# Squared-ReLU attention with top-128 routing on one Trainium2 core: transposing DMAs for two units of each of the last four batches instead of all units of two, and a new hand-written order

## The chip, the cores and the metric

The kernel runs on one core of a Trainium2 chip. The metric is device time in microseconds (us) of one execution; several executions give a median. Engines are named as the profile names them: PE (TensorE matmul), PEld (its weight loads), DVE (VectorE), ACT (ScalarE), POOL (GpSimd), SP (SyncE, which here issues DMAs alone).

## What is computed

Attention for 8 batches, 12 heads, 448 positions and 64 values a head, without a softmax: the scores are scaled, cut off below 0 and squared. Its result, laid out as 448 rows of 768, goes through a layer that treats 128 rows of each batch: those with the highest score against a gate vector.

```python
scores = scale * np.matmul(q, k.transpose(0, 1, 3, 2))
attn = np.maximum(scores, 0.0) ** 2 / S
x = np.matmul(attn, v)                      # then to (B, S, 768)
...
scores = np.einsum('bsd,d->bs', x, w_gate)
out = x.copy()
for b in range(B):
    top_idx = np.argpartition(-scores[b], capacity)[:capacity]   # capacity 128
    xe = x[b, top_idx]
    ye = np.maximum(xe @ w1, 0.0) @ w2
    g = 1.0 / (1.0 + np.exp(-scores[b, top_idx]))
    out[b, top_idx] = x[b, top_idx] + g[:, None] * ye
```

## The kernel before, in words

The work is cut into 24 units of four heads; units 3b, 3b+1 and 3b+2 make batch b. All engines' work is written out by hand in one string, `ORDER` (L535 to L622): each item is a name, a unit or batch, and PSUM banks or an engine. Every engine takes its own items in the order of that string, and waits by itself for the data and buffers that an item needs. PSUM has eight banks; all outputs of PE go through them, so that an item that writes to a bank waits until ACT or DVE has read what stood there.

For unit u:

- `L,q,u`, `L,k,u`, `L,v,u` (L106) load its queries, keys and values from POOL's queue. Six buffers of each kind stand ready. Units that are named in `BYDMA` (L45) are loaded with two DMAs of half the partitions each (L113), in another order of the heads; the others with one (L111).
- `T,u,0` and `T,u,1` (L226) turn queries and keys over on PE, 14 transposes each; `TE,u` (L240) brings both to SBUF, on DVE.
- `S,u,c` for c = 0 to 6 (L256): the scores, four matmuls with 64x64 tiles and 448 columns. `R,u,c` (L264): ReLU of the two banks, always on ACT, 128x896. `Q,u,0` and `Q,u,3` (L270): squares on DVE.
- `V,u,c` (L276): times the values, four matmuls again; `X,u` (L286) brings the result, transposed (768 x 448 for a batch), to `xT_sb`, on ACT or DVE.
- The rows of the output, `x_rows`, are that result turned back. Either `RT,u` does it on PE (L298: 8 transposes of 128x128, or 16 of half the width where a flag says so) and `RE,u` (L307) evicts it on ACT or DVE, or, for units in `BYDMA`, `XB,u` (L314) does it with two transposing DMAs on SP's queue, from SBUF to SBUF, without PE, ACT and DVE.
- `ST,b` (L324) stores a batch's rows from POOL's queue with two DMAs, once all three units of the batch are there.

For a batch b of 0 to 6: `colx`, `colE`, `bt`, `rk`, `cs`, `rank`, `hots`, `sel`, `sE` (L360 to L431) find the 128 rows; `XG` (L443, POOL) gathers them from the stored output, so that it waits for `ST,b`; `XT` and `xeE` turn them over; `h` and `hE` (L481, L492) are the first layer in eight parts, `y` and `yE` (L500, L509) the second; `gs` and `sig` make the gate; `ADD` (L517, POOL) adds to the output in DRAM. Batch 7 takes its rows from `x_rows` in SBUF by matmul (`xe`, L433). Some items have a flag for the width of their tile on PE: `h` and `y` with it do their work as two half tiles of 64 columns.

At the start (`LFq`, `LFk`, L118 and L121) the first queries and keys come by SP's queue in FP32: queries, then 2 of 7 parts of the keys, then the other 5. `Cq` and `Ck` (L201, L204) cast them, `T,0,0` and `TK` (L237) turn them over, `TQE` and `TKE` (L250, L253) bring them to SBUF; all queries go through one PSUM bank. `PW` (L207) are matmuls of zeros that fill PE's time.

Of the kernel before, what the change touches and what calls it, by code (L numbers as in the profile page):

```python
# [21 lines left out]
def kernel(  # L22
# [518 lines left out]
    TE,2,2,D S,2,0,0 R,2,0,A S,2,1,2 R,2,1,A X,0,D S,2,2,4 S,2,3,6 L,q,3 T,3,0,0 Q,1,3,7 T,3,1 TE,3,2,D R,2,2,A
    L,v,1 L,k,4 V,1,0,2 V,1,1 V,1,2 V,1,3 R,2,3,A S,2,4,4 S,2,5,6 S,2,6,0 Q,2,0,3 L,q,4 R,2,4,A V,1,4 V,1,5
    V,1,6 R,2,5,A R,2,6,A T,4,0,4 S,3,0,6 R,3,0,A X,1,D T,4,1 TE,4,2,D L,k,5 Q,2,3,7 S,3,1,0 S,3,2,2 S,3,3,6
    R,3,1,A S,3,4,4 L,v,2 L,q,5 T,5,0,0 T,5,1 R,3,2,A R,3,3,A S,3,5,2 R,3,4,A TE,5,2,D S,3,6,6 V,2,0,4 V,2,1
    L,q,6 R,3,5,A Q,3,0,3 Zk V,2,2 V,2,3 V,2,4 S,4,0,0 R,3,6,A R,4,0,A Q,3,3,7 S,4,1,2 L,k,6 L,k,7 L,v,3 W,0,3,6
    W,0,5,6 V,2,5 V,2,6 R,4,1,A S,4,2,6 X,2,A T,6,0,0 T,6,1 W,0,1,6 R,4,2,A TE,6,2,D RT,0,1,2 colx,0,0,3 S,4,3,4
    RE,0,D colx,0,1 colx,0,2 Q,4,0,3 R,4,3,A Zb colE,0 S,4,4,0 S,4,5,6 L,q,7 RT,1,0,2 RE,1,D R,4,4,A R,4,5,A
    RT,2,0,4 S,4,6,0 bt,0,5 RE,2,D rk,0,2 R,4,6,A L,q,8 L,v,4 Q,4,3,7 S,5,0,6 S,5,1,2 R,5,0,A R,5,1,A V,3,0,0
    rk,0,0 V,3,1 V,3,2 V,3,3 S,5,2,6 R,5,2,A rk,0,3 V,3,4 V,3,5 V,3,6 rk,0,1 L,k,8 X,3,A T,7,0,2 T,7,1 TE,7,2,D
    S,5,3,6 R,5,3,A S,5,4,0 S,5,5,4 cs0,0,6 cs,0,0 cs,0,1 R,5,4,A cs,0,2 Zx,1 rank,0 hots,0 R,5,5,A RT,3,0,7  # L550
    RE,3,D S,6,0,2 S,5,6,0 L,v,5 R,6,0,A sel,0,6 T,8,0,4 T,8,1 R,5,6,A Q,5,0,3 sE,0 S,6,1,2 R,6,1,A TE,8,2,D
    S,6,2,0 V,4,0,6 R,6,2,A V,4,1 V,4,2 V,4,3 S,6,3,2 R,6,3,A V,4,4 V,4,5 S,6,4,4 Q,5,3,7 V,4,6 R,6,4,A X,4,D
    L,k,9 V,5,0,0 V,5,1 Q,6,0,3 S,6,5,2 L,v,6 R,6,5,A V,5,2 V,5,3 S,6,6,4 R,6,6,A ST,0 Q,6,3,7 V,5,4 V,5,5 V,5,6
    X,5,A S,7,0,2 R,7,0,A colx,1,0,6 colx,1,1 S,7,1,4 RT,4,0,7 colx,1,2 R,7,1,A S,7,2,0 L,q,9 T,9,0,2 R,7,2,A
    W,0,4,6 T,9,1 W,1,0,8 colE,1 S,8,0,4 R,8,0,A L,k,10 L,q,10 bt,1,6 TE,9,2,D S,7,3,0 S,7,4,2 R,7,3,A R,7,4,A
    V,6,0,4 Zx,2 V,6,1 V,6,2 V,6,3 S,7,5,0 rk,1,3 R,7,5,A rk,1,0 V,6,4 V,6,5 V,6,6 S,8,1,2 RE,4,D L,q,12 Q,7,0,3
    RT,5,1,7 rk,1,2 rk,1,1 R,8,1,A X,6,A T,10,0,0 S,7,6,2 R,7,6,A XG,0 T,10,1 S,8,2,4 cs0,1,6 cs,1,0 W,0,2,6
    RE,5,D TE,10,2,D cs,1,1 cs,1,2 W,0,0,6 rank,1 XT,0,0,7 R,8,2,A S,8,3,2 R,8,3,A S,8,4,0 S,8,5,4 W,1,6,8 L,v,7
    xeE,0,2,D h,0,0,0,6 h,0,1,0 hots,1 R,8,4,A h,0,2,0 S,8,6,2 h,0,3,0 L,k,12 R,8,5,A R,8,6,A S,9,0,0 S,9,1,4
    Q,7,3,7 h,0,4,0 h,0,5,0 L,v,8 h,0,6,0 h,0,7,0 R,9,0,A R,9,1,A S,9,2,0 R,9,2,A V,7,0,2 Q,8,0,3 V,7,1 V,7,2  # L560
# [118 lines left out]
```

## Time and profile before

| what | us |
|---|---|
| median of 3 runs (197.3 to 199.45) | 197.46 |
| the profiled execution | 197.49 |
| span of its instructions in the trace | 195.8 |
| what lies outside the span | 1.69 |

Times in the trace count from the start of the span. The profile's page has the busy time of each engine, the chain of work that ended last, and the costliest groups of instructions; other views give busy time by stretch (windows), the instructions in order of time (timeline, which merges neighbours of one kind: its start is that of the first, and the step of one is the difference of two starts), and who waited for whom.

### The profile page before, as it was taken

To read this page: it belongs to the slowest core of one execution; us is meant where nothing else is said; L and a number is where in the kernel's file an instruction comes from. 1 tells how busy PE (TensorE), PEld (TensorE's weight loads), DVE (VectorE), ACT (ScalarE), POOL (GpSimd) and SP (SyncE) were. 2 spreads that over 40 slices of the span, in tenths; PEclk is the share of its full clock that TensorE was granted. 3 is DMA by queue.
4 is the path that set the end of the run, shared out by engine and by line. 5 is a ranking of instruction groups with operands and counts; after the bars stand their busy time and mean duration, and the time that the engine had idled before them with its cause. 6 is when DMAs were issued, how large, how long until landed. Compare 5 with 4: busy or idle time off the path is not lost.

```text
span 195.8 us, 7321 instructions
## 1 busy us (share of the span) xinstructions
PE 178.4 (91%) x3221; PEld 125.0 (64%) x3221; DVE 162.0 (83%) x228; ACT 164.4 (84%) x209; POOL 111.1 (57%) x160
## 2 busy tenths in 40 slices
...
GB/s 171 148 186 203 204 209 202 263 282 194 181 197 347 207 99 172 197 299 246 174 167 191 326 149 235 252 130 115 120 133 309 155 272 216 187 79 291 47 125 26
DMA packets 32333, 37.70 MB, mean 193 GB/s; under 512 B 8744, under 2 KB 29614, under 8 KB 31278
## 3 DMA queue, kind: packets, MB, share of 16 engines
...
## 4 chain that ended last, share of the span: by engine, by line
PE 61%; ACT 25%; issue 5%; DVE 4%; POOL 2%; POOLq 0%; DVEq 0%; ACTq 0%
ACT r_sb L216 24%; PE ps L260 12%; PE ps L487 10%; PE ps L505 10%; PE ps L281 9%; PE ps L233 7%; PE ps L295 4%; PE ps L209 2%; PE ps L365 2%; POOL out_dram L523 2%; PE ps L377 1%; DVE a_sb L274 1%; ACT xT_sb L216 1%; DVE qkt L220 1%; DVE mask_sb L388 1%
## 5 line engine op out<-in xcount | busy, mean ns | idle before, releaser
L216 ACT ACTIVATE r_sb<-ps 128x896 bf16<-128x896 f32 x168 | 140.2, 967 | 6.3 <-PE ps L260 5.8
L274 DVE TENSOR_TENSOR a_sb<-r_sb 128x2688 bf16<-128x2688 bf16 (+1 forms) x48 | 84.8, 1784 | 2.7 <-ACT r_sb L216 1.8
L260 PE MATMUL ps<-qkt 64*64 64x448 bf16 x672 | 55.5, 361 | 3.2 <-ACT r_sb L216 2.3
L281 PE MATMUL ps<-a_sb,v_sb 64*64 64x448 bf16 x672 | 41.7, 350 | 0.6 <-ACT r_sb L216 0.4
L260 PEld LDWEIGHTS <-qkt 64*64 64x64 bf16 x672 | 22.1, 104 | 21.1 <-issue 11.0
L220 DVE COPY qkt<-ps 128x1792 bf16<-128x1792 bf16 (+2 forms) x25 | 26.0, 1045 | 2.1 <-PE ps L233 1.6
L281 PEld LDWEIGHTS <-v_sb 64*64 64x64 bf16 x672 | 21.4, 107 | 9.3 <-issue 1.6
L446 POOL DMA_INDIRECT xg<-out_dram,idx x7 | 13.3, 1897 | 22.3 <-DVE idx L430 12.0
L487 PE MATMUL ps<-xeT,w_sb 128*128 128x128 bf16 (+1 forms) x396 | 24.6, 220 | 0.0
L487 PEld LDWEIGHTS <-w_sb 128*128 128x128 bf16 (+1 forms) x396 | 21.9, 98 | 4.0 <-issue 3.1
L505 PE MATMUL ps<-w_sb,hT 128*128 128x384 bf16 (+1 forms) x132 | 24.3, 327 | 0.0
L523 POOL DMA_INDIRECT out_dram<-gye,idx x9 | 17.4, 1929 | 8.6 <-ACT gye L216 6.6
L327 POOL DMA_DIRECT2D out_dram<-x_rows x8 | 4.5, 561 | 28.9 <-DMA x_rows<-xT_sb 9.2
L111 POOL DMA_DIRECT2D v_sb<-in_v_dram x18 | 14.0, 781 | 4.2 <-PE ps L260 1.8
L505 PEld LDWEIGHTS <-hT 128*128 128x128 bf16 (+1 forms) x132 | 11.1, 98 | 8.0 <-issue 2.1
L233 PE MATMUL ps<-ident,q_sb 128*64 128x128 bf16 x336 | 14.3, 225 | 1.6 <-ACT r_sb L216 1.2
L233 PEld LDWEIGHTS <-q_sb 128*64 128x64 bf16 x336 | 11.8, 112 | 6.3 <-issue 5.6
L222 DVE TENSOR_SCALAR xT_sb<-ps 128x896 bf16<-128x896 f32 x12 | 13.1, 1088 | 2.1 <-PE ps L281 1.2
L111 POOL DMA_DIRECT2D q_sb<-in_q_dram x17 | 12.9, 757 | 3.0 <-DVE a_sb L274 1.2
L233 PE MATMUL ps<-ident,k_sb 128*64 128x128 bf16 x336 | 14.1, 221 | 0.0
L111 POOL DMA_DIRECT2D k_sb<-in_k_dram x17 | 12.6, 741 | 2.2 <-PE ps L260 1.4
L216 ACT ACTIVATE xT_sb<-ps 128x896 bf16<-128x896 f32 x12 | 11.7, 975 | 0.8 <-PE ps L281 0.8
(122 smaller groups left out, 200.4 us busy)
## 6 DMA issues: line engine op xcount, KB each, us to landing
...
```

The lines of the kernel that those rows point to most:

```text
L111: nc.gpsimd.dma_start(out=dst, in_=src(t, u))
L216: nc.scalar.activation(out=out_, in_=in_, func=func or AF.Copy, scale=scale)
L220: nc.vector.tensor_copy(out=out_, in_=in_)
L222: nc.vector.tensor_scalar(out=out_, in0=in_, scalar1=scale, scalar2=None, op0=ALU.mult)
L233: nc.tensor.matmul(out=PSB[HALF[j], at["T", u, w], n * 128:(n + 1) * 128], lhsT=s[:, j, c, :], rhs=ident, is_transpose=True, start=(n == 0 ...
L260: nc.tensor.matmul(out=PS[HALF[hf], bank + j, :S], lhsT=qkt[u][HALF[j], 1, c, hf, :], rhs=qkt[u][HALF[j], 0, :, hf, :], start=True, stop=True)
L274: nc.vector.tensor_tensor(out=a_sb[u][:, c0:c1], in0=r, in1=r, op=ALU.mult)
L281: nc.tensor.matmul(out=PS[HALF[j], at["V", u] + hf, :S], lhsT=v_sb[u % NBUF][HALF[hf], j, c, :], rhs=a_sb[u][HALF[hf], c, j, :], start=(c ...
L446: read = reads[self.b] = nc.gpsimd.indirect_dma_start(out=self.xg, out_offset=None, in_=out[0:self.b + 1].rearrange("b s d -> (b s) d"), i ...
L487: nc.tensor.matmul(out=PS[p, self.at["h"] + bk, o:o + 128], lhsT=w1_sb[:, m, f * 128 + p.start:f * 128 + p.stop], rhs=self.xeT[:, m, :], s ...
L505: nc.tensor.matmul(out=PS[p, self.at["y"] + w, :384], lhsT=self.hT[:, f, p], rhs=w2_sb[:, f, w * 384:(w + 1) * 384], start=(f == 0), stop= ...
L523: add = nc.gpsimd.indirect_dma_start(out=out[0:self.b + 1].rearrange("b s (w d) -> (b s w) d", w=w), out_offset=bass.IndirectOffsetOnAxis( ...
```

## The change

Eight units instead of six have their rows turned by DMA: the first two of each of batches 4 to 7 (12, 13, 15, 16, 18, 19, 21, 22), where before all of batches 5 and 6 did (15 to 20). The units in `BYDMA` are also those that are loaded by halves. The first queries are turned over into two PSUM banks: five of seven parts into one, two into another, and the two are evicted apart, the first on ACT. Of the loads by SP the first keys now come ahead of the queries. The whole order is written anew, with other banks, other engines for some evictions, and other places for half tiles.

```diff
-    BYDMA = (15,16,17,18,19,20)
+    BYDMA = (12,13,15,16,18,19,21,22)
...
+    NA = 5
...
+        if (u, w, n0) == (0, 0, 0):
+            n1 = NA
+        o = NA if (u, w, n0) == (0, 0, NA) else 0
         for n in range(n0, n1):
             c = n // 2 + NR * (n % 2) if w == 0 else n
             for j in range(2):
-                nc.tensor.matmul(out=PSB[HALF[j], at["T", u, w], n * 128:(n + 1) * 128],
+                nc.tensor.matmul(out=PSB[HALF[j], bank if o else at["T", u, w], (n - o) * 128:(n - o + 1) * 128],
                                  lhsT=s[:, j, c, :], rhs=ident, is_transpose=True,
-                                 start=(n == 0), stop=(n == NC - 1), skip_group_check=True)
+                                 start=(n == o), stop=(n == n1 - 1 if (u, w) == (0, 0) else n == NC - 1),
+                                 skip_group_check=True)
+
+    def TB(bank):
+        at["TB"] = bank
+        T(0, 0, bank, NA, NC)
...
-            put(eng, flat[:, w, n0 * 128:n1 * 128], PSB[:, at["T", u, w], n0 * 128:n1 * 128])
+            own = (u, w, n0) == (0, 0, NA)
+            put(eng, flat[:, w, n0 * 128:n1 * 128],
+                PSB[:, at["TB"], :(n1 - n0) * 128] if own else PSB[:, at["T", u, w], n0 * 128:n1 * 128])
...
-    Zz PW,32,0 Zi Zs LFq Cq,0 Zt LFk,0,2 Zm Ck,0,2,D Cq,1 T,0,0,0 TK,0,2 LFk,2,7 TQE,0,7,D Ck,2,7,D TKE,0,2,A
+    Zz PW,32,0 Zi Zs LFk,0,2 Zh Zt Zm LFq Cq,1 Cq,0 LFk,2,7 PW,6,1 T,0,0,0 Lw TB,2 Ck,0,2,D TK,0,2 TQE,0,5,A
+    TQE,5,7,D TKE,0,2,D PW,5,3 S,0,0,2 S,0,1,4 L,q,1 R,0,0,A L,k,1 Ck,2,7,D TK,2,7 TKE,2,7,D PW,8,6 S,0,2,0 Zc
...
```

What the new order moves is shown by the built program, engine by engine. First DVE's queue at the start, before and now (qf and kf are the first queries and keys as loaded, q_sb and k_sb their casts, qkt both turned over, ps is PSUM):

```order
L220 CAST q_sb_85<-qf 128x448
L220 CAST k_sb_91<-kf 128x2x128
L220 COPY qkt<-ps 128x896
L220 CAST k_sb_91<-kf 128x2x320
L187 CAST ident_f<-ident 128x128
L220 COPY qkt<-ps 128x640
```

```order
L188 CAST ident_f<-ident 128x128
L221 CAST q_sb_85<-qf 128x448
L221 CAST k_sb_91<-kf 128x2x128
L221 COPY qkt<-ps 128x256 x2
L221 CAST k_sb_91<-kf 128x2x320
L221 COPY qkt<-ps 128x640
```

The one copy of all queries (896 wide) is gone from DVE; it has two of 256 instead, the last two parts of the queries and the first two of the keys.

Then ACT's queue up to the ReLUs of unit 11, before and now (r_sb is what the ReLUs write, xT_sb what `X` writes, hT what `hE` writes):

```order
L216 ACTIVATE q_sb_85<-qf 128x448
L216 ACTIVATE qkt<-ps 128x256
L216 ACTIVATE r_sb<-ps 128x896 x30
L216 ACTIVATE xT_sb_103<-ps 128x2x448
L216 ACTIVATE r_sb<-ps 128x896 x8
L216 ACTIVATE xT_sb_104<-ps 128x2x448
L216 ACTIVATE r_sb<-ps 128x896 x11
L216 ACTIVATE xT_sb_104<-ps 128x2x448
L216 ACTIVATE r_sb<-ps 128x896 x8
L216 ACTIVATE xT_sb_105<-ps 128x2x448
L216 ACTIVATE r_sb<-ps 128x896 x11
L216 ACTIVATE xT_sb_105<-ps 128x2x448
```

```order
L217 ACTIVATE q_sb_85<-qf 128x448
L217 ACTIVATE qkt<-ps 128x640
L217 ACTIVATE r_sb<-ps 128x896 x40
L217 ACTIVATE xT_sb_104<-ps 128x2x448
L217 ACTIVATE r_sb<-ps 128x896 x8
L217 ACTIVATE xT_sb_104<-ps 128x2x448
L217 ACTIVATE r_sb<-ps 128x896 x9
L217 ACTIVATE xT_sb_105<-ps 128x2x448
L217 ACTIVATE r_sb<-ps 128x896 x9
L217 ACTIVATE hT<-ps 128x1024
L217 ACTIVATE r_sb<-ps 128x896 x4
L217 ACTIVATE xT_sb_105<-ps 128x2x448
```

Of the evictions `X` one fewer stands on ACT among the first 70 ReLUs, and one `hE` has come there.

Last ACT's queue at the end, before and now (x_rows is what `RE` writes, g the gate, gye what `yE` writes):

```order
L216 ACTIVATE x_rows<-ps 128x4x256
L479 ACTIVATE g__3045<-ps 128x1
L216 ACTIVATE r_sb<-ps 128x896 x4
L216 ACTIVATE x_rows<-ps 128x4x256
L216 ACTIVATE xT_sb_104<-ps 128x2x448
L216 ACTIVATE x_rows<-ps 128x4x256
L216 ACTIVATE hT<-ps 128x1024
L216 ACTIVATE xeT<-ps 128x256
```

```order
L217 ACTIVATE r_sb<-ps 128x896 x7
L217 ACTIVATE xT_sb_104<-ps 128x2x448
L490 ACTIVATE g__3056<-ps 128x1
L217 ACTIVATE xeT<-ps 128x768
L217 ACTIVATE x_rows<-ps 128x4x256
L217 ACTIVATE hT<-ps 128x1024
L217 ACTIVATE xeT<-ps 128x512
```

The evictions of rows of units 21 and 22 are gone here, as are their `RT` on PE; unit 23's is left.

## Rows read from the trace of the kernel before

**Rows 1.** The page: busy time of the engines, and the chain by engine

```profile
PE 178.4 (91%) x3221; PEld 125.0 (64%) x3221; DVE 162.0 (83%) x228; ACT 164.4 (84%) x209; POOL 111.1 (57%) x160
...
PE 61%; ACT 25%; issue 5%; DVE 4%; POOL 2%; POOLq 0%; DVEq 0%; ACTq 0%
```

**Rows 2.** Windows: stretch, length, then busy us (xcount) of each engine

```profile
6.40:71.90 65.50, 59.72 (x1155) 39.57 (x1156) 62.60 (x83) 65.07 (x81) 38.98 (x58) 1.00 1.17 214
71.90:165.00 93.10, 91.98 (x1712) 64.98 (x1715) 86.05 (x119) 86.58 (x111) 55.90 (x74) 1.00 1.16 201
165.00:185.10 20.10, 20.10 (x299) 15.13 (x288) 11.17 (x22) 9.16 (x13) 7.63 (x9) 1.00 0.71 156
185.10:195.80 10.70, 1.33 (x12) 0.61 (x10) 0.16 (x1) 1.16 (x2) 3.23 (x5) 0.73 0.56 74
```

**Rows 3.** Timeline of PE, 99 to 109 us: start, us, what, count

```profile
99.08 0.61 PE L295 MATMUL ps<-ident,xT_sb 128*128 128x128 bf16 x8
99.62 0.38 PE L260 MATMUL ps<-qkt 64*64 64x448 bf16 x4
99.83 0.55 PE L281 MATMUL ps<-a_sb,v_sb 64*64 64x448 bf16 x8
...
102.64 0.58 PE L233 MATMUL ps<-ident,q_sb 128*64 128x128 bf16 x14
103.03 0.58 PE L233 MATMUL ps<-ident,k_sb 128*64 128x128 bf16 x14
...
107.32 1.18 PE L487 MATMUL ps<-xeT,w_sb 128*128 128x128 bf16 x18
108.44 0.38 PE L260 MATMUL ps<-qkt 64*64 64x448 bf16 x4
```

**Rows 4.** Timeline at 72 us: the transposes of unit 6's rows

```profile
71.89 0.61 PE L295 MATMUL ps<-ident,xT_sb 128*128 128x128 bf16 x8
```

**Rows 5.** DMA issues: engine, count, KB each, us from issue to landing

```profile
qf<-in_q_dram SPq DMA_DIRECT2D x1, 448.0 KB, 3.2
...
kf<-in_k_dram SPq DMA_DIRECT2D x1, 128.0 KB, 3.1
```

**Rows 6.** Timeline of the first 7 us

```profile
0.81 0.46 SPq L119 DMA_DIRECT2D qf<-in_q_dram  x1
...
4.08 0.55 DVE L220 CAST q_sb<-qf 128x448 bf16<-128x448 f32 x1 [3.07 <-DMA qf<-in_q_dram]
4.55 0.75 DVE L220 CAST k_sb<-kf 128x256 bf16<-128x256 f32 x1
...
4.69 0.98 PE L233 MATMUL ps<-ident,q_sb 128*64 128x128 bf16 x14
...
5.91 0.38 ACT L216 ACTIVATE qkt<-ps 128x256 bf16<-128x256 bf16 x1 [1.26 <-PE ps L233]
...
6.38 0.57 PE L260 MATMUL ps<-qkt 64*64 64x448 bf16 x8
```

**Rows 7.** Line L320: transposing DMAs (SP's ns for one; landing), then L111's whole loads

```profile
L320 SPq DMA_TRANSPOSE x_rows<-xT_sb x12: 1190/1276/3841, 126.0 to 154.0; - x12
...
DMA to landing us min/median/max: 3.5/4.8/9.0
...
DMA to landing us min/median/max: 4.4/8.7/10.0
```

**Rows 8.** Waits: POOL's longest wait for transposing DMAs

```profile
POOL out_dram L327 <- DMA x_rows<-xT_sb: 9.2, 1, 9.2
```

**Rows 9.** Timeline of the last stage, batch 7: X, RT and RE of unit 22, xe

```profile
167.27 1.08 DVE L222 TENSOR_SCALAR xT_sb<-ps 128x896 bf16<-128x896 f32 x1
...
168.82 0.61 PE L295 MATMUL ps<-ident,xT_sb 128*128 128x128 bf16 x8
...
169.47 1.02 ACT L216 ACTIVATE x_rows<-ps 128x1024 bf16<-128x1024 bf16 x1 [1.41 <-PE ps L295]
...
176.56 1.51 PE L438 MATMUL ps<-hot__3775,x_rows 128*128 128x128 bf16 x24
```

More of the change, by code (lines that the diff above doesn't have):

```diff
@@ L541 @@
[L541 to L560, printed above, removed]
@@ new lines @@
+    S,3,1,6 R,3,0,A S,3,2,0 R,3,1,A R,3,2,A S,3,3,2 R,3,3,A V,2,0,4 V,2,1 S,3,4,6 Zk Q,2,3,7 L,q,7 S,3,5,0
+    R,3,4,A R,3,5,A V,2,2 V,2,3 Q,3,0,3 V,2,4 V,2,5 V,2,6 W,0,1,6 S,3,6,2 R,3,6,A X,2,D L,k,5 T,5,0,6 L,k,6
+    T,5,1 S,4,0,0 R,4,0,A S,4,1,4 S,4,2,2 L,q,9 R,4,1,A TE,5,2,D S,4,3,6 Zx,0 L,q,6 RT,0,0,0 R,4,2,A RT,2,0,1
+    L,v,5 colx,0,0,4 colx,0,1 R,4,3,A S,4,4,2 Q,3,3,7 RT,1,0,5 R,4,4,A S,5,0,6 R,5,0,A RE,0,D RE,2,D colx,0,2
+    Q,4,0,3 S,5,1,0 L,k,7 colE,0 T,6,0,2 S,5,2,6 T,6,1 R,5,1,A R,5,2,A RE,1,D S,4,5,0 bt,0,4 L,q,8 S,4,6,6
@@ new lines @@
+    R,4,5,A R,4,6,A S,5,3,0 TE,6,2,D V,3,0,2 V,3,1 V,3,2 R,5,3,A S,5,4,6 V,3,3 V,3,4 R,5,4,A V,3,5 V,3,6 S,5,5,0
+    L,k,8 X,3,A rk,0,0 L,q,10 W,0,0,6 cs0,0,5 rk,0,1 cs,0,0 rk,0,2 cs,0,1 cs,0,2 L,k,9 T,8,0,6 T,8,1 L,v,4
+    Q,4,3,7 rk,0,3 rank,0 hots,0 R,5,5,A S,5,6,2 TE,8,2,D R,5,6,A S,6,0,4 R,6,0,A T,7,0,0 T,7,1 S,6,1,2 S,6,2,6
+    Q,5,0,3 R,6,1,A R,6,2,A TE,7,2,D S,6,3,4 V,4,0,2 V,4,1 R,6,3,A V,4,2 V,4,3 L,v,6 ST,0 S,6,4,6 R,6,4,A
+    S,6,5,0 R,6,5,A V,4,4 L,k,11 W,0,5,6 Q,5,3,7 sel,0,4 colx,1,0,5 V,4,5 V,4,6 V,5,0,6 V,5,1 V,5,2 sE,0 V,5,3
@@ new lines @@
+    V,5,4 Q,6,0,3 X,4,A S,6,6,0 L,k,12 R,6,6,A V,5,5 V,5,6 X,5,D L,k,10 S,7,0,2 RT,3,0,4 S,7,1,0 colx,1,1
+    colx,1,2 RE,3,D colE,1 R,7,0,A S,7,2,2 R,7,1,A S,7,3,6 T,9,0,4 T,9,1 Q,6,3,7 TE,9,2,D R,7,2,A S,7,4,0
+    R,7,3,A R,7,4,A bt,1,2 rk,1,0 rk,1,3 S,7,5,6 S,7,6,0 R,7,5,A W,0,2,6 R,7,6,A V,6,0,4 V,6,1 rk,1,1 V,6,2
+    S,8,0,6 V,6,3 V,6,4 V,6,5 R,8,0,A V,6,6 X,6,A L,v,7 S,8,1,0 R,8,1,A rk,1,2 S,8,2,2 XG,0 T,10,0,6 T,10,1
+    W,0,4,6 RT,4,1,4 Q,7,0,3 TE,10,2,D XT,0,1,5 xeE,0,2,D S,8,3,0 RE,4,D S,8,4,6 R,8,2,A R,8,3,A S,8,5,2
@@ new lines @@
+    colx,2,0,2 colx,2,1 TE,12,2,D W,1,6,8 colx,2,2 W,1,1,8 sel,1,3 colE,2 R,10,0,A sE,1 R,10,1,A gs,0,4 sig,0
+    L,k,13 S,10,2,6 R,10,2,A S,10,3,2 S,10,4,0 Q,9,3,7 RT,8,0,4 bt,2,5 RE,8,D rk,2,0 ST,1 W,1,5,8 R,10,3,A
+    R,10,4,A rk,2,2 rk,2,3 S,11,0,6 W,1,0,8 rk,2,1 V,9,0,2 V,9,1 W,1,2,8 V,9,2 V,9,3 V,9,4 S,11,1,0 V,9,5 V,9,6
+    R,11,0,A R,11,1,A S,11,2,6 X,9,D R,11,2,A RT,7,0,4 RE,7,D W,1,4,8 RT,6,0,5 RE,6,D S,10,5,0 S,10,6,6
+    y,0,0,2,0,2 W,1,3,8 W,1,7,8 y,0,1,2,0 R,10,5,A R,10,6,A cs0,2,4 cs,2,0 cs,2,1 cs,2,2 rank,2 hots,2 y,0,2,2,0
```

135 lines of the change are left out of this document (68 added, 67 removed).

## The prediction

> **What bounds the kernel now.** I read the page first. PE is busy 91% of the span, ACT 84%, DVE 83%, and the chain that ended last lies 61% on PE and 25% on ACT [rows 1]. Such shares are a mean over stages, so the windows come next [rows 2]. From the first scores (6.4 us) to 71.9 us ACT is busy 65.1 of 65.5 us, with 81 instructions: 0.80 us each, one after the other. From there to 165 PE is busy 92.0 of 93.1 us, and to 185.1 all the time; ACT has 9.2 of 20.1 us left to do in that last stretch. So there are two stages, one that ACT sets and one that PE sets. A busy PE is not yet a PE at its pace, so I took steps from start to start in PE's timeline [rows 3]. Rows of a unit (eight transposes) are followed after 0.54 us by scores, and one S (four matmuls) after 0.21 by V; the 14 transposes of the queries take 0.39 to those of the keys; three parts of `h` with the change of tile shape behind them take 1.12. I read these as: S and V 0.19 each, T 0.39, RT 0.45, one part of `h` 0.335, and 0.1 for a change between tiles of 64x64, 64-wide and full width.
>
> With such steps PE's own list can be summed. Up to the transposes of unit 6, which start at 71.89 [rows 4], it has 77 S and 63 V (26.6 us), 25 T (9.8), 7 RT (3.2), 8 parts of `h` (2.7), 9 `colx`, 2 `bt` and small items (5.3 together) and 62 changes of shape (6.2): 53.8 us. But 65.5 us pass from the first S at 6.38 [rows 6] to there: PE waits for 11.7 us. Ahead of the same point ACT has 75 ReLUs and 5 evictions `X`, 80 x 0.797 = 63.8 us. So 10.0 of the 11.7 us are ACT's work less PE's work, and 1.7 are other waits. From there to batch 7's `y` PE's list has 108.1 us of work and takes 111.6: only 3.5 us of waiting in that whole stage. These two facts carry the forecast. The first stage ends when ACT lets it end; after it, PE's work is the time.
>
> **The change, part by part.** The sum is made against the profiled execution: span 195.8, its own time 197.49, which is the median of the runs (197.46) within 0.03 us.
>
> *Start.* The queries are now issued by SP behind the first keys. Before, SP took 0.46 us for the first issue at 0.81, and the queries landed 3.2 us after it [rows 5, 6]. Issued at 1.3 they land at 4.5 instead of 4.06. The keys' DMA, with under a third of the bytes, took 3.1 us [rows 5], so size counts for little: I take 0.45 us later, with bounds of 0 (had the two shared their time) and 0.6. In return the eviction of the queries no longer waits for all 14 transposes. Before, it was 1.69 us from the first transpose (4.69) to the first S (6.38) [rows 6]. Now 10 of the 14 must be done (0.98 x 10/14 = 0.70), then ACT copies 640 columns. The trace shows 0.38 us for 256 on ACT [rows 6] and 1.02 for 1024 [rows 9]; between them by width that is 0.70. This makes about 1.5. The other branch is DVE's: the cast of the keys (0.75) stands behind that of the queries (0.55), and two copies of 256 follow, the second over by 1.85 at the latest if DVE takes as long as ACT. I take 1.65, so that the first S and with it ACT's first ReLU come 0.4 us later (bounds -0.2 and +0.75).
>
> *First stage.* ACT is full there, so what it does ahead of PE's tightest point counts. In the new list that point is S of unit 10, part 6, which needs the bank of ReLU 2 of unit 11. ACT's work ahead of it is 78 ReLUs and 4 X (82 x 0.797 = 65.4) and one `hE` of 0.92 beside a gate of under 0.1: 66.3. PE's work ahead of it is 79 S and 70 V (28.3), 25 T (9.8), 9 RT (4.1), 8 parts of `h` (2.7), 9 `colx`, 3 `bt`, XT and small items (6.0) and 62 changes of shape (6.2): 57.1. The difference is 9.2 instead of 10.0. One eviction X fewer on ACT and one batch's evictions better placed make 0.8 us less waiting; I take 0.7. It is hidden by nothing, since both engines stand against each other here. The bounds are 0 (if DVE, busy 62.6 of these 65.5 us [rows 2], takes over as the limit) and -2.4 (if the other 1.7 us of waits went too).
>
> *Second stage.* Two RT fewer in all (16 units instead of 18): 2 x 0.45 = 0.9 us of PE. Two changes of shape fewer: 0.2. Against it, ten more parts of `h` and eight more parts of `y` run as half tiles; no row here isolates their price. If the halves only add instructions it is near 0.02 each (0.4 in all), at worst a whole change of shape each (1.8); I take 0.45, near the lower end, since a half tile next to another needs no change. Seven more PW (0.2) fall in the first stage where PE waits. PE's balance is -0.65 us, and here it is on the path. The two RE that go (1.02 each on ACT in the last stage [rows 9], where ACT is idle half of the time [rows 2]) are worth nothing there.
>
> *Two more units by transposing DMA.* Four more DMAs on SP, which does nothing else, and 0 on PE. The six more half loads cost POOL some issue time; POOL is busy 57% [rows 1] and its queue is long ahead, which covers it. If that cover is gone, V or T waits for its load. *Tail.* The 10.7 us behind 185.1 [rows 2] hold the same adds and evictions: 0.
>
> Sum: +0.4 - 0.7 - 0.65 = -0.95 us on 197.49, so 196.5; the late waits of 3.5 us I leave as they are, with a slight lean to fewer since the last stretch lost RT and RE of units 21 and 22: **196.4 us**.
>
> [...] Transposing DMAs landed 3.5 to 9.0 us after their issue, whole loads 4.4 to 10.0, and a store waited 9.2 us for transposed rows [rows 7, 8]. [...]
>
> **Rivals.**
>
> 1. *Transposed rows land late: slower.* Batch 7 now takes two units' rows by DMA, and `xe` on PE needs them. Between the end of V of unit 22 and `xe` the new list has eight parts of `y` (2.6), eight of `h` (2.7), V of unit 23 (1.3), six `g` (1.1), three `colx` (0.6), XT, RT and small items (1.1) and three changes (0.3): 9.7 us. [...] Batches 5 and 6 have the same risk one step earlier, since their stores wait for such rows, gathers for the stores, and `XT` on PE for the gathers: 9.0 instead of 4.8 at one of them is up to 4.2 us less some cover. [...] For it: the wait of 9.2 us. Against it: in the old trace that wait reached no engine but POOL, and loads are few behind 165 us.
> 2. *Nothing gained.* DVE, busy 62.6 of 65.5 us and 86.1 of 93.1 [rows 2], meets the new order worse: two X more stand on it and Q at other places. If the 0.7 of ACT becomes a wait for DVE, and half tiles cost 0.9 more, it is 196.4 + 1.3 = about 197.7.
> 3. *More gained.* The 1.7 us of other waits in the first stage and half of the 3.5 us later were places of the old order; a new order may have neither. With the start at no loss as well that is up to 196.4 - 0.4 - 1.7 - 1.7 = 192.6; half of it makes 194.5. Against it: 3.5 us in 111.6 is little already.
> 4. *The change doesn't do what it says.* ACT, not PE, could set the pace to the end, so that RT on PE is worth nothing. Rows 2 speak against it (86.6 of 93.1, then 9.2 of 20.1); it would come out near 197.0 and is counted with rival 2.
>
> **How the numbers follow.** A measurement of this kernel tells about 1% from no change, 2.0 us: faster means below 195.5, slower above 199.4. Forecast 0.38 (195.5 to 197.2), rivals 2 and 4 together 0.20 (to 199), rival 3 0.26, rival 1 0.16. Rival 3 lies mostly below 195.5 and the forecast's low edge adds a little: faster 0.30. Rival 1 gives slower, in part just under the line: 0.16. Same has the rest, 0.54. The range reaches from halfway into rival 3 to where rival 1 begins: 194.0 to 199.6, with one in ten outside on either side.
>
> **What would show it.** Right: ACT's first ReLU near 7.2 us instead of 6.8; ACT still full up to 70 us or so, with its tightest point in units 10 and 11; then PE full; 16 groups of row transposes on PE; batch 7's first `y` near 182.5; and no wait of PE for a DMA. Wrong: gaps of PE ahead of `xe` or `XT` with a DMA as releaser (rival 1), DVE named ahead of S or V (rival 2), or PE's waiting behind 72 us well under 3 us (rival 3).

## The result: slower by 1%, with a spread of 7 us

| | kernel before | kernel after |
|---|---|---|
| median of 20 runs | 197.34 us | 201.77 us |
| from, to | 196.66 to 200.13 | 197.85 to 204.78 |
| the profiled execution, its span | 197.49, 195.8 | 199.98, 198.3 |

The ratio after to before is 1.0104, 95% interval 1.007 to 1.0139; it takes only the runs of each kernel within 1.5% of its fastest, the medians take all. The forecast was 196.4 us, range 194.0 to 199.6, with 0.16 for slower.

First the page of the kernel after: busy time of the engines [rows 1], the granted clock in 40 slices, the queue that brings instructions, and the chain by engine.

```profile
PE 179.2 (90%) x3270; PEld 125.3 (63%) x3270; DVE 158.3 (80%) x227; ACT 165.5 (83%) x209; POOL 115.8 (58%) x166
...
PEclk9999999999999999999999999997999999999995
...
q8 instruction: 25, 0.41, 0.8%
...
PE 64%; ACT 19%; issue 7%; DVE 3%; DMA 2%; POOL 2%; SPq 0%; DVEq 0%; POOLq 0%; ACTq 0%
```

Three things are new. One slice near 138 us has a clock of 7 tenths. "Issue", time in which an engine waits for nothing that the profile shows, is up from 5 to 7% of the chain, and ACT's share is down from 25 to 19%. Then windows by stage (columns as in [rows 2]; behind the engines stand the granted clock, the busy share of the DMA engines and the GB/s that they moved):

```profile
7.30:72.00 64.70, 59.14 (x1179) 40.03 (x1179) 61.51 (x82) 64.18 (x80) 40.36 (x61) 1.00 1.19 218
72.00:133.00 61.00, 60.01 (x1136) 41.42 (x1133) 57.39 (x78) 57.67 (x72) 38.69 (x55) 1.00 1.19 207
133.00:135.80 2.80, 1.96 (x44) 1.47 (x45) 1.92 (x4) 1.73 (x3) 0.54 (x1) 1.00 0.83 108
135.80:139.20 3.40, 3.40 (x19) 2.12 (x18) 3.40 (x10) 2.91 (x4) 3.40 (x4) 0.50 0.18 13
139.20:165.00 25.80, 25.63 (x500) 17.46 (x497) 20.47 (x30) 23.15 (x30) 12.83 (x16) 1.00 1.06 218
```

The first stage is as before: ACT full, 80 instructions in 64.2 us. But PE stands for 1.0 us in 72 to 133, for 0.84 in 133 to 135.8, and then works 3.4 us at half the clock (granted 0.50 from 135.8 to 139.2). PE's timeline at the two places:

```profile
90.96 0.38 PE L271 MATMUL ps<-qkt 64*64 64x448 bf16 x4
91.27 0.38 PE L376 MATMUL ps<-wg_col,xT_sb 128*128 128x1 bf16 x9
92.61 0.51 PE L376 MATMUL ps<-wg_col,xT_sb 128*128 128x1 bf16 x15 [0.96 <-issue]
...
132.93 0.75 PE L376 MATMUL ps<-wg_col,xT_sb 128*128 128x1 bf16 x24
134.52 0.27 PE L436 MATMUL ps<-tok,hot__2598 128*128 128x2 bf16 x4 [0.84 <-issue]
134.72 0.76 PE L271 MATMUL ps<-qkt 64*64 64x448 bf16 x12
135.41 0.75 PE L388 MATMUL ps<-ident_f,cols 128*128 128x128 f32 x4
135.96 1.06 PE L306 MATMUL ps<-ident,xT_sb 128*128 128x128 bf16 x8
136.81 2.99 PE L516 MATMUL ps<-w_sb,hT 128*128 128x384 bf16 x10
```

`colx` of a batch is 24 equal matmuls in three items. After nine of them PE stands for 1 us, between the first and the second matmul of an item, which read one tile and write one bank; the trace names nothing that it waits for there ("issue", 0.96 us). At 133.5 it stands again, and 1.3 us after it goes on its clock halves: eight transposes of `RT` take 0.85 us from their start to the next start instead of 0.45 (at 94.25 us of the same trace), and ten matmuls of `y` 2.99 (1.79 in a_noh64, without the stop, below).

The account, from items' starts in both traces: first scores 0.92 later (6.38, 7.30); PE's waits up to the first stage's tightest point 0.55 less (11.68, 11.13); PE's listed work 0.84 less; waits and half clock behind that point 2.62 more (3.60, 6.22); the end behind the last `y` 0.34 longer. The sum is +2.49, the difference of the spans. So the gains of the forecast came (0.55 and 0.84), the later start and the longer end took 1.26 us of them back, and the 2.62 us behind the tightest point made the kernel slower.

### The profile page after: what moved, and what is told of

Read it like the earlier page. It is cut to its first block, busy times and chain, and to the rows that moved or that the text cites. A ratio compares the mean times of both kernels' runs of the same rounds, so it can differ in the third digit from the quotient of the medians.

```text
span 198.3 us, 7453 instructions
## 1 busy us (share of the span) xinstructions
PE 179.2 (90%) x3270; PEld 125.3 (63%) x3270; DVE 158.3 (80%) x227; ACT 165.5 (83%) x209; POOL 115.8 (58%) x166
## 3 DMA queue, kind: packets, MB, share of 16 engines
q1 hardware_dynamic: 9550, 3.02, 11.2%
## 4 chain that ended last, share of the span: by engine, by line
PE 64%; ACT 19%; issue 7%; DVE 3%; DMA 2%; POOL 2%; SPq 0%; DVEq 0%; POOLq 0%; ACTq 0%
ACT r_sb L217 17%; PE ps L271 14%; PE ps L292 12%; PE ps L498 12%; PE ps L516 11%; PE ps L237 6%; PE ps L306 4%; PE ps L376 2%; DMA qf<-in_q_dram 2%; POOL out_dram L534 2%; PE ps L388 1%; DVE qkt L221 1%; DVE a_sb L285 1%; ACT xT_sb L217 1%; PE ps L485 1%
## 5 line engine op out<-in xcount | busy, mean ns | idle before, releaser
L457 POOL DMA_INDIRECT xg<-out_dram,idx x7 | 14.0, 2006 | 27.8 <-DVE idx L441 23.0
L516 PE MATMUL ps<-w_sb,hT 128*128 128x384 bf16 (+1 forms) x148 | 25.2, 337 | 0.0
L516 PEld LDWEIGHTS <-hT 128*128 128x128 bf16 (+1 forms) x148 | 11.9, 104 | 8.4 <-issue 3.2
L223 DVE TENSOR_SCALAR xT_sb<-ps 128x896 bf16<-128x896 f32 x14 | 15.2, 1086 | 1.5 <-PE ps L292 1.2
L112 POOL DMA_DIRECT2D q_sb<-in_q_dram x15 | 11.2, 751 | 7.9 <-PE ps L237 5.9
L112 POOL DMA_DIRECT2D v_sb<-in_v_dram x16 | 13.4, 836 | 3.8 <-DMA out_dram<-x_rows 1.6
L237 PEld LDWEIGHTS <-q_sb 128*64 128x64 bf16 x336 | 11.2, 110 | 6.8 <-issue 4.1
L217 ACT ACTIVATE xT_sb<-ps 128x896 bf16<-128x896 f32 x10 | 9.8, 976 | 3.5 <-PE ps L292 3.5
L112 POOL DMA_DIRECT2D k_sb<-in_k_dram x15 | 11.1, 742 | 1.9 <-DMA q_sb<-in_q_dram 1.2
```

The lines of the kernel that those rows point to most:

```text
L112: nc.gpsimd.dma_start(out=dst, in_=src(t, u))
L217: nc.scalar.activation(out=out_, in_=in_, func=func or AF.Copy, scale=scale)
L223: nc.vector.tensor_scalar(out=out_, in0=in_, scalar1=scale, scalar2=None, op0=ALU.mult)
L237: nc.tensor.matmul(out=PSB[HALF[j], bank if o else at["T", u, w], (n - o) * 128:(n - o + 1) * 128], lhsT=s[:, j, c, :], rhs=ident, is_tran ...
L457: read = reads[self.b] = nc.gpsimd.indirect_dma_start(out=self.xg, out_offset=None, in_=out[0:self.b + 1].rearrange("b s d -> (b s) d"), i ...
L516: nc.tensor.matmul(out=PS[p, self.at["y"] + w, :384], lhsT=self.hT[:, f, p], rhs=w2_sb[:, f, w * 384:(w + 1) * 384], start=(f == 0), stop= ...
```

## What PE stands for: its own instructions

The page counts 25 transfers on the instruction queue, 0.41 MB: 16 KB each (16384 bytes in the trace). PE has 3270 matmuls and as many weight loads, some 262 instructions for each transfer. Counted in the trace (with the 24 other entries of PE's queue), PE stands in after behind instructions 3265 and 4801 and in before once, behind 4033: the distances are 6 x 256 and 3 x 256, and no other divisor of 768 is as near to the 262 of a transfer. So by this trace PE's list comes in blocks of 256, with cuts at fixed places in it. The stop of before, in `colx` too:

```profile
113.49 0.20 PE L365 MATMUL ps<-wg_col,xT_sb 128*128 128x1 bf16 x2
114.42 0.70 PE L365 MATMUL ps<-wg_col,xT_sb 128*128 128x1 bf16 x22 [0.73 <-issue]
```

The trace keeps each of these transfers with its time. This is my own table from these records and PE's starts (us; "PE at the next cut" is the start of the last instruction ahead of the cut; a_bad, a_same, a_plain and b_h2 are kernels of the experiments below):

```
kernel   PE enters  transfer of the    PE at the  PE goes  behind the  stands
         a block    next from .. to    next cut   on at    transfer
before    108.44    111.99 .. 112.94    113.52    114.42     1.48       0.89
after      86.66     90.21 ..  91.10     91.49     92.61     1.51       1.13
after     128.05    131.60 .. 133.10    133.52    134.52     1.42       1.00
a_bad     147.63    151.91 .. 152.84    152.30    154.10     1.26       1.80
a_same    148.35    152.64 .. 153.81    153.58    155.38     1.58       1.80
a_plain    87.61     91.48 ..  92.37     92.46     93.73     1.36       1.27
b_h2      148.40    150.20 .. 152.26    152.38    153.74     1.47       1.36
```

In 236 of 257 cases behind 72 us in the 16 traces the transfer for the next block starts after PE has entered the block ahead of it, in the others up to 1.6 us earlier. It takes about 1 us (0.9 to 2.2), and PE goes on some 1.45 us behind its end (1.26 to 1.58 in the table), which I count as the arrival. From entering a block to the next one's arrival it took 5.0 us in the median of both kernels between 75 and 165 us (2.5 to 7.6). PE takes 4.8 to 9.3 us for a block of the kernel after. Where PE was through a block before the arrival, it stood for the difference (last column). By these times no more than one block lay ready ahead of the one that PE was in.

My theory A then was: blocks of many short instructions, of which the new order has more (half tiles of `h` need twice the instructions for the same 0.34 us: five parts at 85.46 us of after take 60 matmuls and 1.70 us; `colx` and `T` lie near them), come late while the DMA engines are full (a share of 1.19 from 72 to 133 us); a stop may bring the half clock. Its rivals: B, the transposes and half loads delay the data; C, the clock falls for the amount of work in the new order.

## The experiments

The kernel before has medians of 197.14 to 197.97 us on the chips used, so each median stands beside that of the kernel before on the same chip. A dash: too few comparable runs for a ratio.

| kernel | median us | before | difference | ratio, 95% interval |
|---|---|---|---|---|
| after (20 runs) | 201.77 | 197.34 | +4.4 | 1.0104 (1.007 to 1.0139) |
| a_good | 200.02 | 197.97 | +2.1 | 1.0105 (1.0066 to 1.0144) |
| a_bad | 203.18 | 197.97 | +5.2 | 1.0267 (1.0204 to 1.0329) |
| b_bad | 198.43 | 197.97 | +0.5 | 1.0022 (0.9979 to 1.0065) |
| a_qfirst | 201.00 | 197.97 | +3.0 | - |
| a_noh64 | 197.84 | 197.86 | 0.0 | 1.0004 (0.9983 to 1.0025) |
| b_h64 | 198.24 | 197.86 | +0.4 | 1.0021 (0.9988 to 1.0054) |
| a_noload | 195.77 | 197.86 | -2.1 | 0.9889 (0.986 to 0.9917) |
| a_noh64_q | 197.74 | 197.86 | -0.1 | 0.9984 (0.9956 to 1.0011) |
| a_same | 201.03 | 197.14 | +3.9 | 1.0198 (1.0173 to 1.0222) |
| a_plain | 198.85 | 197.14 | +1.7 | 1.0089 (1.0058 to 1.0119) |
| a_stop | 203.28 | 197.14 | +6.1 | 1.031 (1.0261 to 1.0358) |
| a_best | 197.26 | 197.14 | +0.1 | 1.0012 (0.9989 to 1.0036) |
| a_best2 | 198.05 | 197.61 | +0.4 | 1.0009 (0.9974 to 1.0043) |
| b_h2 | 201.18 | 197.61 | +3.6 | - |

**The cuts moved, nothing else (a_good, a_bad, b_bad).** `PW` got a width, so that fewer wide or more narrow matmuls of zeros fill the start for the same time.

a_good against after:

```diff
-    PW,32,0
+    PW,8,0,512
...
-    PW,6,1
+    PW,1,1,512 PW,1,1,256
...
-    PW,8,6
+    PW,2,6,512
```

a_bad against after:

```diff
-    PW,32,0
+    PW,2,0 PW,60,0,64
```

b_bad against before:

```diff
-    PW,32,0
+    PW,6,0 PW,52,0,64
```

a_good: 

> The kernel after, with 34 fewer of the matmuls of zeros ahead of the first unit, those left being wider, so that PE is filled as long as before: every later instruction of PE stands 68 places earlier in its list, and nothing else changes. Theory A (late instructions: PE's instructions come by DMA in blocks of 16 KB, 256 instructions; the next block is asked for as PE enters one and comes 4.4 to 5.8 us later in the middle half of the traced cases, since the DMA engines are full; PE stands still where it runs through a block faster): the new cuts fall where PE takes longer for a block. The stops of 1.1 us in colx of batch 3 (91.5 us) and of 1.0 us between colx of batch 5 and sel of batch 4 (133.5 us) are gone, no half clock at 136 to 139 us; by the traced block times stops behind 72 us sum to 0.8 us instead of 1.45 in the mean. Median 197 to 199, where the kernel after has 201.8. Theory B (the eight more transposing issues and the half loads delay the data themselves) and theory C (the clock falls for the amount of work in the new order): the place in the list means nothing, 200 to 203 as before, with the same stops.

a_bad: 

> The kernel after, with 30 more matmuls of zeros at the start, each of half the width: every later instruction of PE stands 60 places later. Theory A: the cuts fall badly, into blocks that PE runs through in 4.5 us (ends at about 90.4 and 150.3 us) and 5.2 us (70.1); mean sum of stops behind 72 us 1.8 us instead of 1.45, so stops of about 1 us near 90 and 150 us, none at 133 us, and a median of 201.5 to 204. Theories B and C: as the kernel after, stops at the same instructions as there.

b_bad: 

> The kernel before, with 26 more matmuls of zeros at the start (52 of half the width for 26): every later instruction of PE stands 52 places later. Theory A: the cuts come to blocks that PE runs through in 5.1 us at 106.6 and at 152.5 us and 5.5 us at 112; mean sum of stops behind 72 us 1.2 us instead of 0.8; median 197.7 to 199 instead of 197.3, spread more like that of the kernel after. Theories B and C: 197.3, no change.

a_bad stood where it was said, at 90.1 and 152.3 us, and nowhere else for over 0.75 us behind 72; the second stop and its half clock in PE's timeline:

```profile
152.00 0.46 PE L376 MATMUL ps<-wg_col,xT_sb 128*128 128x1 bf16 x13
154.11 0.23 PE L376 MATMUL ps<-wg_col,xT_sb 128*128 128x1 bf16 x3 [1.64 <-issue]
...
155.38 1.06 PE L388 MATMUL ps<-ident_f,cols 128*128 128x128 f32 x4
```

In a_good both stops of after are gone; but two new ones stand at new cuts (87.3 and 149.2 us, 1.2 and 1.5 us, both between two transposes of one `T`), so that it stayed a microsecond over what was expected. Its median is 2.4 us nearer to before than that of after, but its ratio (1.0105) is the same as that of after (1.0104): what went is the upper part of the spread (highest 201.65 instead of 204.78). a_bad's ratio, 1.0267, lies clear above after's: there the place of the cuts alone costs time. b_bad fell into its range, but the interval holds no change: it decides nothing. The stops follow the cuts, not the instructions: B and C fall as causes of the stops. a_same, the same list as after, stood at 73.8 and 155.4 us instead of 92.6 and 134.5: again at cuts, but at others, since the arrivals vary (2.5 to 7.6 us, above).

**Fewer instructions, or fewer transfers (a_noh64, b_h64, b_h2, a_noload, a_plain).** The flag of `h` is its fourth number; a_noh64 clears the twelve that are set, b_h64 sets the same twelve in before, b_h2 eleven, of which four (batch 4) are the same.

a_noh64 against after (b_h64 is the reverse, in before):

```diff
-    h,0,5,1 h,0,6,1 h,0,7,1
+    h,0,5,0 h,0,6,0 h,0,7,0
...
-    h,1,3,1 h,1,4,1 h,1,5,1 h,1,6,1 h,1,7,1
+    h,1,3,0 h,1,4,0 h,1,5,0 h,1,6,0 h,1,7,0
...
-    h,4,4,1 h,4,5,1 h,4,6,1 h,4,7,1
+    h,4,4,0 h,4,5,0 h,4,6,0 h,4,7,0
```

b_h2 sets the flag of `h` 1 to 7 of batch 2 and 4 to 7 of batch 4 in before. a_same is the kernel after itself. a_noload against after, in the loop over `ORDER`:

```diff
+            if name == "L" and args[1] >= 14:
+                continue
```

a_plain against after, in `XB`:

```diff
-            nc.sync.dma_start_transpose(
-                out=x_rows[b][:, :, 128 * m:128 * m + 128],
-                in_=xT_sb[b % NX][:, m].rearrange("p c n -> p (c n)"))
+            nc.sync.dma_start(out=x_rows[b][:, :, 128 * m:128 * m + 128], in_=xT_sb[b % NX][:, m])
```

a_noh64: 

> The kernel after, with the 12 parts of h that ran as half tiles (72 instruction pairs more than whole ones) as whole tiles again; the rest of its order and flags as they are. Theory A (late instructions): h by halves needs twice the instructions for the same 0.34 us, so PE runs through its blocks faster than they come; without it the mean sum of stops behind 72 us, worked out from the block times of the list and the 130 traced arrivals, falls from 1.6 to 0.4 us, for 0.3 us more of changes of tile shape. Few or no stops near 1 us, no half clock between 72 and 190 us in most runs: median 197.5 to 199.5 beside 201.8 for the kernel after. Theory B (the transposing and half transfers as such): 200 to 203, since all of them stay.

b_h64: 

> The kernel before, with the same 12 parts of h run by halves as in the kernel after. Theory A: block times of 5.0 and 4.3 us appear (ends near 104 and 148 us); mean sum of stops behind 72 us 2.1 us instead of 1.0, 0.4 us of work more, and half-clock stretches as in the kernel after: 199.5 to 203, with a spread like that of the kernel after. Theory B: 197.5 to 198.3, since no transfer changes.

a_noload: 

> The kernel after without the loads of queries, keys and values of units 14 to 23; these units work on what older units left in the buffers. PE's list of instructions is the same to the last one; what falls is the traffic of the DMA engines behind 75 us. Theory A: instruction blocks come in some 3 us instead of 5, so behind 80 us no stop at a cut and no half clock until the end: the 4 us of waits and half clock of that stretch in the profiled run go, 195.5 to 197.5 with little spread. Theory C (the clock falls for the amount of PE's work): half clock as before, since PE works as much or more closely: 199 to 202.

a_same: 

> The kernel after once more, beside the three below on one chip. Theory A: median 200.5 to 203 with a spread of some us; its stops of 0.5 us and more behind 72 us lie only where a new block of 256 instructions begins, and differ in number and place from the first trace, since the arrivals vary.

a_plain: 

> The kernel after with plain copies in place of the 16 transposing DMAs (same bytes, same queue, same waits; the rows stored for the eight units are not turned). Theory A alone (loads keep the DMA engines full): blocks still come in some 5 us, stops and spread as in the kernel after, within 0.7 us of its median. Theory A with a part for the transposes (in the kernel after and its two variants the blocks asked for between 141 and 151 us, among four transposes, took 4.9 to 7.4 us; in the kernel before 3.3 to 4.8 us): there they come in 3 to 4.5 us, the stops near 150 us go, those near 90 us stay: 1 to 2.5 us less than the kernel after. Theory B (the transposes are the cause): 196.5 to 198, no stops.

b_h2: 

> The kernel before with 11 other parts of h by halves, all of batch 2 and half of batch 4 (the 12 of the kernel after cost it only 0.4 us). Theory A with all traced arrivals taken as equally likely everywhere: blocks of 4.25 us (ending near 107 us) and 5.0 us (112) and 4.2 us (149), stops of 2.8 us in the mean behind 72 us against 1.0, so 199.5 to 202. Theory A by place (arrivals in three kernels with the order of before: 3.2 to 5.9 us at 101 to 108, and 3.3 to 4.0 us at 147 to 149, where this order has no run of four transposes): a stop of about 0.6 us in the mean at 107 and none at 149, 198 to 199.5. If halves cost nothing but with the transposes: 197.1 to 197.7.

a_noh64 is the whole change without its half tiles of `h`, and it is as quick as before (nine of ten runs 197.4 to 198.3). PE's timeline at the two old places:

```profile
91.09 0.75 PE L376 MATMUL ps<-wg_col,xT_sb 128*128 128x1 bf16 x24
...
131.97 0.75 PE L376 MATMUL ps<-wg_col,xT_sb 128*128 128x1 bf16 x24
132.58 0.27 PE L436 MATMUL ps<-tok,hot__2550 128*128 128x2 bf16 x4
...
134.42 1.79 PE L516 MATMUL ps<-w_sb,hT 128*128 128x384 bf16 x10
```

All 24 of `colx` run through, and no stretch of half clock stands ahead of 185 us. Its waits behind the tightest point are 3.64 us, those of before 3.60. Taking out instructions moves the cuts too, but this is more than a lucky place of them: slid over every place of the list between 72 and 165 us, with the stops at cuts taken out, 256 instructions take less than 5.0 us at 10% of the places in after, at 4% in before and at 0.2% in a_noh64 (shortest 4.3, 4.5 and 4.8 us). Small stops stay: at the cut near 114 us the four kernels with whole tiles and no added wait stand 0.2 to 0.6 us.

b_h64 was a miss: +0.4 where 1.5 to 5 were expected, and no stop over 0.75 us at a cut. Its quickest block (4.3 us) ended at 151.7, and in this run the next had come in 4.0. In these traces half tiles did harm only where a cut followed them and the block was late. b_h2 put seven of them elsewhere and got +3.6 us by the medians (four runs, 198.7 to 203.55). PE's timeline of b_h2, a whole `h` by halves and a stop in the scores behind it:

```profile
105.04 1.53 PE L487 MATMUL ps<-xeT,w_sb 128*64 128x128 bf16 x48
106.50 0.38 PE L260 MATMUL ps<-qkt 64*64 64x448 bf16 x2
107.65 0.57 PE L260 MATMUL ps<-qkt 64*64 64x448 bf16 x6 [0.78 <-issue]
```

48 matmuls in 1.5 us are 96 instructions; the block took 4.1 us, and the next came 5.3 us after PE had entered it. So the halves did it in the old order too, without the new transposes. The half of that expectation that went by the place of earlier arrivals (none at 149) failed: PE also stood at 152.4, behind the same four parts as in b_h64, since this time the next block took 5.3 us to come.

a_noload keeps PE's list to the last instruction and takes traffic away: DMA share 0.53 instead of 1.19 from 72 to 133 us, blocks in 3.4 us in the median, no stop at a cut over 0.75 us, no half clock, and 2.1 us quicker than before. Its windows:

```profile
72.00:133.00 61.00, 60.25 (x1152) 41.88 (x1152) 57.57 (x77) 57.88 (x72) 13.17 (x16) 1.00 0.53 122
133.00:140.00 7.00, 7.00 (x118) 4.73 (x118) 6.83 (x15) 6.52 (x9) 5.61 (x5) 1.00 0.49 130
140.00:165.00 25.00, 24.76 (x482) 17.44 (x478) 21.07 (x29) 23.14 (x30) 7.49 (x11) 1.00 0.77 153
```

That is against C: PE works as much here (60.25 us of the first 61, in after 60.01). The transposes have a part: a_plain moves the same bytes unturned and is 2.2 us quicker than a_same on the same chip (four runs each, 198.03 to 199.48 and 200.68 to 201.65). The rows of SP's queue are "q1 hardware_dynamic" in both pages, first the kernel after, then a_plain:

```profile
q1 hardware_dynamic: 9550, 3.02, 11.2%
```

```profile
q1 hardware_dynamic: 9294, 3.02, 6.5%
```

By these pages the packets of the same 3.02 MB took 11.2% of the span of 16 engines turned and 6.5% unturned. The five blocks that follow those entered from 121 to 151 us came in 5.7 us in the mean in after and in a_same, in 5.0 in a_plain and in 4.6 in before, each from one trace. PE's timeline of a_plain has no stop near 153 but keeps the one near 92:

```profile
92.25 0.38 PE L374 MATMUL ps<-wg_col,xT_sb 128*128 128x1 bf16 x9
93.73 0.51 PE L374 MATMUL ps<-wg_col,xT_sb 128*128 128x1 bf16 x15 [1.11 <-issue]
...
153.69 0.60 PE L386 MATMUL ps<-ident_f,cols 128*128 128x128 f32 x4
154.22 0.57 PE L271 MATMUL ps<-qkt 64*64 64x448 bf16 x8
```

So in these traces blocks come later with the transposes, and short instructions make PE reach the cut earlier. Plain copies take away part of the loss (1.0089 stays); whole tiles take away all of it (1.0004), with the transposes in place.

**A wait put in by hand (a_stop).** On a_noh64:

```diff
+    def Zd():
+        for _ in range(6):
+            nc.vector.tensor_tensor(out=dz, in0=dz, in1=dz, op=ALU.mult)
+    def PD(bank):
+        nc.tensor.matmul(out=PS[:, bank, :128], lhsT=zero, rhs=dz[:, :128], start=True, stop=True,
...
-    colx,5,1 colx,5,2 colE,5 sel,4,5
+    colx,5,1 colx,5,2 Zd colE,5 PD,5 sel,4,5
```

> The kernel after with whole tiles in h (197.84 us, no stop over 0.25 us behind 72 us), and one wait put in by hand: six multiplications of zeros on DVE (about 2 us) ahead of colE of batch 5, and one matmul of zeros on PE that waits for them ahead of sel of batch 4, near 132 us. If the half-clock stretch in the kernel after was brought by the stop of PE and not by the late block as such, a wait for another engine does the same: half clock for some us beginning about 2 us behind the wait, and the time rises by more than the wait itself: 2 us of wait and up to 1.7 of half clock, 200 to 202. If only the wait counts: 199 to 200.

PE's timeline:

```profile
132.68 0.75 PE L386 MATMUL ps<-wg_col,xT_sb 128*128 128x1 bf16 x24
136.31 0.22 PE L249 MATMUL ps<-dz,zero 128*128 128x128 bf16 x1 [2.89 <-DVE dz L246]
...
137.62 1.11 PE L398 MATMUL ps<-ident_f,cols 128*128 128x128 f32 x4
```

The wait became 2.9 us instead of 2, and half clock ran from 136.8 to 140.2 us, from 0.5 us behind the wait. The time rose by 6.1 us over before by the medians and by 5.0 in this profiled run (202.15 against 197.14); the wait and 1.7 us of half clock make 4.6. DVE's lost time and what queues behind it is in the rest, which this run doesn't part. In this trace a wait for DVE is followed by half clock as a late block was in after.

**The start, and the repairs together (a_qfirst, a_noh64_q, a_best, a_best2).**

a_qfirst against after, and a_noh64_q against a_noh64:

```diff
-    LFk,0,2 Zh Zt Zm LFq Cq,1 Cq,0
+    LFq LFk,0,2 Zh Zt Zm Cq,1 Cq,0
```

a_best is a_noh64_q with `XB,15` and `XB,16` in each other's places; a_best2 against a_best:

```diff
-    LFk,2,7 PW,6,1 T,0,0,0
+    LFk,2,7 T,0,0,0
```

a_qfirst: 

> The kernel after, with the first queries issued ahead of the first keys again, as before the change. In the kernel after the queries landed 1.3 us later than before (5.37 against 4.06) and the first scores started 0.92 us later (7.30 against 6.38). Expected of every theory: queries land near 4.1, first scores at 6.0 to 6.5; the time falls by 0.5 to 1.2 us against the kernel after. Theory A adds that the stops and half-clock stretches behind 72 us stay, and with them most of the spread: 199 to 202.

a_noh64_q: 

> The kernel after with both repairs: whole tiles in the 12 parts of h, and the first queries issued ahead of the first keys. Theory A: 0.5 to 0.9 us less than the kernel with whole tiles alone: 196.8 to 199, the best of the versions, at or under the kernel before. Theory B: 199.5 to 202.

a_best: 

> The kernel after with whole tiles in h, the first queries ahead of the first keys, and the transposes of units 15 and 16 in the order in which their data come (15 before 16, so that 15 need not wait for 16 and four in a row become two and two). Against the version with the first two alone (197.74): the same to 0.5 us less: 197.2 to 197.8; against the kernel before 0 to 0.6 us less. A larger gain would need fewer changes of block while the DMA engines are full, and no theory promises it here.

a_best2: 

> The kernel after with whole tiles in h, the queries first, the transposes of units 15 and 16 in the order of their data, and now also without the six matmuls of zeros ahead of the first transposes. With the queries first these six are in the way: in that kernel the cast of the queries was done at 4.63 us, but PE's 38 matmuls of zeros ran until 5.3 and the first transposes began at 5.23, the first scores at 6.66 (6.78 in the kernel with all repairs). Expected: transposes at about 4.7, first scores at 6.1 to 6.3, and since ACT is full from there on the whole half microsecond stays: 196.4 to 197.0 where the kernel before has 197.1 and the version with the six 197.26. If the late start is not worth anything in the end (first scores earlier, but PE waits for it again before 72 us): 197.1 to 197.4.

The start in the timelines, first the kernel after, then a_qfirst, then a_best2:

```profile
1.34 0.45 SPq L120 DMA_DIRECT2D qf<-in_q_dram  x1
...
5.38 0.49 DVE L221 CAST q_sb<-qf 128x448 bf16<-128x448 f32 x1 [3.72 <-DMA qf<-in_q_dram]
...
5.92 0.70 PE L237 MATMUL ps<-ident,q_sb 128*64 128x128 bf16 x14 [0.61 <-DVE q_sb L221]
...
7.30 0.57 PE L271 MATMUL ps<-qkt 64*64 64x448 bf16 x8 [0.18 <-ACT qkt L217]
```

```profile
4.06 0.57 DVE L221 CAST q_sb<-qf 128x448 bf16<-128x448 f32 x1 [2.41 <-DMA qf<-in_q_dram]
...
5.24 0.74 PE L237 MATMUL ps<-ident,q_sb 128*64 128x128 bf16 x14
...
6.66 0.57 PE L271 MATMUL ps<-qkt 64*64 64x448 bf16 x8 [0.19 <-ACT qkt L217]
```

```profile
4.72 0.82 PE L237 MATMUL ps<-ident,q_sb 128*64 128x128 bf16 x14
...
6.22 0.57 PE L271 MATMUL ps<-qkt 64*64 64x448 bf16 x8 [0.18 <-ACT qkt L217]
```

Behind the keys the queries took 4.0 us to land instead of 3.2 [rows 5]. With the queries first they are cast at 4.63, but PE is held by its own filler until 5.24; without six of the fillers the first scores come at 6.22, as expected. In time the order of the loads shows little: a_qfirst's four runs (197.43 to 201.52) decide nothing, and a_noh64_q is 0.1 us under a_noh64 where 0.5 to 0.9 was expected. The time of a_best2 didn't follow: the half microsecond is still there at the tightest point of units 10 and 11 (74.83 us, a_best 75.33), but its profiled run waits for DVE 0.9 us at 170 and 0.5 at 143, and its ratio to before holds no change. No version beats before clearly; a_best and a_noh64_q equal it and keep all transposes of the change.

## Why the prediction was wrong

*Start.* Forecast +0.4 (bounds -0.2 and +0.75), traced +0.92. The step that "size counts for little", which put the landing at 4.5 us, was off: behind the keys it was 5.3 here. The eight kernels with this head began their scores at 6.4 to 7.6 us, 7.0 in the mean, the four with the old one at 6.1 to 6.5, 6.3 in the mean, so +0.7 is the fairer figure, just inside the bounds. From the transposes to the scores it was 1.38, forecast 1.5 to 1.65.

*First stage.* Forecast 0.7 us less waiting, measured 0.55 less, with ACT full to the forecast point. Right.

*Second stage, PE's work.* Forecast -0.65; over the whole list it is 0.84 less. Right in size, and worth nothing in the end.

*Tail.* Forecast 0, on the ground that the same adds and evictions stand there; traced +0.34. From the start of the last `y` to the end it takes 9.9 to 10.1 us in all kernels with the new order but a_noload (8.8), and 9.6 to 9.8 in those with the old one. Why stays open.

*The step that failed* is the price of the half tiles: "if the halves only add instructions it is near 0.02 each (0.4 in all), at worst a whole change of shape each (1.8)". I priced an added instruction by PE's time for it. No row showed that price; by PE's own time it was not far off: four parts by halves take 1.46 us to the next start in b_h2 (above), three whole ones 1.12 [rows 3], with a change of shape behind both. The price was in the transfer of the list: without the twelve parts of `h` as halves the change stands at 1.0004 of before (a_noh64), with them at 1.0104 and 1.0198 (after, a_same), or +4.4 and +3.9 us by the medians. With it fell "the late waits of 3.5 us I leave as they are": with half clock they became 6.2 in the profiled run and up to 8.5 in a_bad, and with the same list 3.7 in a_noload and 4.1 in a_plain. The sign that I passed over stood in the old trace: the stop of 0.9 us inside `colx` at 113.5, with "issue" as its cause.

*What is left.* Without the half tiles the change still gains nothing: 1.0004 (0.9983 to 1.0025), and 0.9984 (0.9956 to 1.0011) with the queries first, where -0.95 us would be 0.9952. Start and end, each some 0.3 us worse than forecast, take 0.6 of the 0.95; the rest isn't parted.

*Rival 1* named late transposed rows. In the profiled run they cost PE nothing; in a_good `xe` stood 0.9 us for them, in a_noh64 0.2. Its transfers did make things late, but PE's instructions instead of its data (blocks in 5.7 us in the mean, in a_plain 5.0, above). *Rival 2*, DVE: in the profiled run S stood for DVE 0.7 us in all (0.2 before), the two longer times in the first stage (19.1 and 31.2 us); the first stage came out as forecast all the same. In its own sum 0.7 and 0.9 make 1.6, so 198.0 and not 197.7. *Rival 3* wanted half of the late waits gone; the late blocks made them more. *Rival 4*: no; PE set the pace.

*What shows would be right or wrong:* ACT full to 70 us and 16 groups of row transposes came; ACT's first ReLU came at 7.73 instead of 7.2, the first `y` of batch 7 at 185.55 instead of 182.5, and the two gaps of PE over 0.25 us behind 72 us were ended by "issue", which none of the listed signs named.

Open: why a block takes 2.5 us at one time and 7.6 at another; why half clock follows some stops and not others; and the 0.34 us at the end, which wasn't tried.
